# Adding x to the mixed sums on GpSimd alone, from batch 3 on

## The chip, the cores and the metric

One core of one Trainium2 chip runs the kernel. The metric is the device time of one execution in microseconds (us). The engines are named as the profile names them: PE (TensorE, matmuls), PEld (its weight loads), DVE (VectorE), ACT (ScalarE), POOL (GpSimd) and SP (SyncE, which here only issues DMAs). POOL issues DMAs too.

## What is computed

```python
batch, n_heads, seq, head_dim = (8, 12, 448, 64)            # d_model 768, hidden 3072
scores = scale * np.matmul(q, k.transpose(0, 1, 3, 2))
attn = np.maximum(scores, 0.0) ** 2 / S
x = np.matmul(attn, v)                                       # heads side by side: [8, 448, 768]
mixed = np.real(fft(fft(x, axis=1), axis=2))
u = x + mixed
un = (u - mean(u)) / np.sqrt(var(u) + 1e-06)
out = u + np.maximum(un @ w_ch1, 0.0) @ w_ch2
```

The change touches one line of this, `u = x + mixed`.

## The kernel before

Everything runs on one core, batch by batch, with the stages of neighbouring batches laid into one another so that PE always has something to do.

- **Attention** (`attention`, L834). For each batch PE makes scores (L954, in visits of six matmuls), ACT takes relu of them into `sq` (L967), DVE or ACT squares (L984 or L981), and PE multiplies by v (L822, L827). The result leaves PSUM as `xT` (L686 on ACT or L689 on DVE), and a DMA transpose (L796) makes `xn`, with tokens on partitions. q and k are loaded by POOL (L476, L451), copied by DVE (`qkr`, L583) and turned by SP's DMA transposes (`qkT`, L593). From batch 3 on there is one buffer of q and one of k.
- **Mixing** (`mix`, L1416; `mix_rows`, L1228). DVE folds `xT` by the symmetry of the transform (L760 to L780), PE multiplies with the channel table (L1432), and `mix_rows` does the sequence part, once for each of two chunks of a batch. A chunk is two matmuls (L1240) that give a sum's two halves. ACT copies one half (`qs`, L1252), DVE forms `tp = a + b` and `qs = a - b` (L1255, L1257). These are the parts of two rows of tokens: row 0 is the upper half of the sequence, row 1 its mirror image. For each row the inner function `rows(i)` adds x in two instructions, L1275 for the first 385 columns and L1277 for the other 383, which the mirrored part of the other sum gives. So a chunk has four additions, each 112 or 113 partitions of float32 from two SBUF operands. Before the change row 0 is added on DVE and row 1 on POOL. Then follow the statistics on DVE (L1284, L1285), the root on ACT (L1287), the reciprocal on DVE (L1289, L1290) and the normalised row `un` on ACT (L1303) or POOL (L1300).
- **Stores.** Row 0 goes to DRAM as `utop` and `ntop` from SP (L1338), row 1 as `ubot` and `nbot` by indirect DMAs from POOL (L1341). A row's `u` has one buffer from batch 1 on (`BU`), which comes free when `un` has been made and `u` stored.
- **FFN** (`ffn`, L1874; `joint`, L1733). The normalised rows come back transposed as `unT` (L1380, issued by SP) in groups of 256 tokens. Groups 2 to 7 run L1930 (first product, relu by L1917 on ACT or L1915 on DVE) and L1985 or L2071 (second product, added to u by DVE's L1623). The last four groups run as two joints of two groups each: L1762, with copies by ACT (L1777), sums by DVE (L1782), then L2071. The tokens of group 3 are the last 64 of batch 2 and the first 192 of batch 3.

**What sets the order.** The order on each engine is fixed when the program is built. Every stage is a generator that asks for an engine, a modelled duration, what it waits for and which buffers it takes; `Streams.run` (L102) gives the next place to the stage that could start first, and its rank breaks ties. It keeps one clock for each engine. A duration of type `Port` on POOL also makes a DVE `Port` instruction longer while it runs. So one changed duration or engine shifts all later choices: the order of PE, whether a relu goes to ACT or DVE, the place of a load on POOL. On the chip each engine runs its list strictly in that order.

`WHOLE` is 3 (L215). Below it the two additions of a row are placed as one piece, from it on as two (`next_step`, L218).

Of the kernel before, what the change touches and what calls it, by code (L numbers as in the profile page):

```python
# [149 lines left out]
def need(eng, dur, deps=(), bufs=(), ok=None):  # L150
    return eng, dur, list(deps), list(bufs), ok
# [6 lines left out]
def act(n):  # L158
    return n / 1200 + (0.17 if STAGE[0] else 0.2)


def dve(n):
    return n / 960 + 0.15
# [14 lines left out]
def kernel(  # L178
# [9 lines left out]
    nc = tc.nc  # L188
# [9 lines left out]
    KN = D // 2 + 1  # L198
# [16 lines left out]
    WHOLE = 3  # L215
    JOINTS = list(range(8, NGR, 2))

    def next_step(b, eng, d, e):  # L218

        return e if b < WHOLE else (yield need(eng, d))  # L220
# [752 lines left out]
    def sooner(t, other, d, usual, du):  # L973

        wait = {en: max(t, sch.engine[en]) + sch.queued(en) for en in (other, usual)}
        return wait[other] + d + SPARE < wait[usual] + du
# [18 lines left out]
    def side(b, ch):  # L995

        return ch if b < ONE else 1
# [202 lines left out]
    def turn_rows(un, t, n, idn, c0, w, en, done):  # L1200

        e = yield need("PE", 6 * 0.06, [t], [BS])
        pt = BS.take()
        for m in range(MC):
            nc.tensor.matmul(pt[:, m // 3, m % 3 * 128:m % 3 * 128 + w], lhsT=un[:n, m * 128:(m + 1) * 128],
                             rhs=idn, start=True, stop=True)
        if done is second_un[0]:
            BUN[0].free.append(e)
        e = yield need(en, (act if en == "ACT" else dve)(6 * w), [e + LATENCY["PE"]])
        (nc.scalar.copy if en == "ACT" else nc.vector.tensor_copy)(  # L1210
            groups[1][2][:, :, c0:c0 + w].rearrange("p (h m) w -> p h m w", h=2),
            pt[:, :, 0:384].rearrange("p h (m w) -> p h m w", w=128)[:, :, :, 0:w])
        BS.give(pt, e)
        done.t = e + LATENCY["ACT"]
# [13 lines left out]
    def mix_rows(b, ch, pcs):  # L1228
# [38 lines left out]

        def rows(i):

            eng, en, d = ((nc.vector, "DVE", 2 * dve(KN)), (nc.gpsimd, "POOL", 1.8))[i]  # L1270
            one = b < WHOLE
            e1 = yield need(en, Port(d if one else d / 2), [e + LATENCY["DVE"]] + x_ready[b], [BU[i][side(b, ch)]])
            x = xns[b][:, 2 * i + ch, :]
            u = us[i] = work.tile([128, D], FP32, name="u", tag=("u", "u1")[i] + "AB"[side(b, ch)], bufs=1)
            eng.tensor_tensor(u[:n, 0:KN], ts[i][:n, 0:KN], x[:n, 0:KN], op=ALU.add)  # L1275
            e1 = yield from next_step(b, en, Port(d / 2), e1)
            eng.tensor_tensor(u[:n, KN:D], ts[1 - i][:n, KN - 2:0:-1], x[:n, KN:D], op=ALU.add)  # L1277
            made_u[i].t = e1 + LATENCY[en]
            e1 = yield need("DVE", 2 * dve(D // 2) + 0.2 if one else dve(D // 2), [made_u[i]])
            stats = work.tile([128, 2, 6], FP32, name="stats", tag="stats", bufs=2)  # L1280
            for hf in range(2):
                if hf:
                    e1 = yield from next_step(b, "DVE", dve(D // 2) + 0.2, e1)
                nc.vector.bn_stats(stats[:n, hf, :], u[:n, hf * (D // 2):(hf + 1) * (D // 2)])  # L1284
            nc.vector.bn_aggr(mv[:n, i, :], stats[:n])  # L1285
            e1 = yield need("ACT", 0.25, [e1 + LATENCY["DVE"]])
            nc.scalar.activation(std[:n, i:i + 1], mv[:n, i, 1:2], AF.Sqrt, bias=eps_t[:n])  # L1287
            e1 = yield need("DVE", 0.3, [e1 + LATENCY["ACT"]])
            nc.vector.reciprocal(rstd[:n, i:i + 1], std[:n, i:i + 1])  # L1289
            nc.vector.scalar_tensor_tensor(nmr[:n, i:i + 1], mv[:n, i, 0:1], -1.0, rstd[:n, i:i + 1],  # L1290
                                           op0=ALU.mult, op1=ALU.mult)
            if i == 0:
                taken.t = yield need("SP", 0.0, [e1], [BUN[ch if b < ONE else 0]])
            yield need("SP", 0.0, [e1, taken])
            e1 = max(e1, taken.t) + LATENCY["DVE"]
            en = "ACT" if b == 1 or sooner(e1, "ACT", act(D) - 1.0, "POOL", 1.05) else "POOL"
            e1 = yield need(en, act(D) if en == "ACT" else Port(1.05), [e1])
            un = work.tile([128, D], BF16, name="un", tag=f"un{2 * (ch if b < ONE else 0) + i}", bufs=1)
            if en == "POOL":
                nc.gpsimd.tensor_scalar(un[:n], u[:n], rstd[:n, i:i + 1], nmr[:n, i:i + 1],  # L1300
                                        op0=ALU.mult, op1=ALU.add)
            else:
                nc.scalar.activation(un[:n], u[:n], AF.Identity, bias=nmr[:n, i:i + 1],  # L1303
                                     scale=rstd[:n, i:i + 1])
            uns[b][2 * ch + i] = un
            freed[i].t = e1
            made_un[i].t = e1 + LATENCY[en]
            if b == 1:
                nr, idn, c0, w = ((128, ident, 64, 128), (128, rev[:, 0:127], 64 + HS + 97, 127),
                                 (96, ident[:96, :96], 64 + 128, 96), (97, rev[:97, 31:128], 64 + HS, 97))[2 * ch + i]  # L1310
                sch.add(turn_rows(un, e1 + LATENCY[en], nr, idn, c0, w, ("DVE", "ACT")[i],
                                  second_un[1 + 2 * ch + i]), (1, 0.1))

        for i in range(2):
            sch.add(rows(i), rank)
# [899 lines left out]
```

## Time and profile before

| | us |
|---|---|
| three runs | 566.94, 569.09, 569.48 |
| their median | 569.09 |
| the profiled execution: its span | 566.4 |
| of the span, idle on PE | 9.9 |

The profile gives the profiled execution's span, from its first instruction to its last, and no other time for it. The fastest of the three runs lies 0.5 us above that span.

The profile has a page with busy times by engine, groups of equal instructions with the mean time of one, the idle time ahead of them and what ended it. Beside it there are views of the waits (which engine waited for which line), of stretches of time (busy time of each engine in each), of one line's instructions (shortest, median and longest) and a timeline. A time in a timeline counts from the start of the span. The end of a matmul is modelled, so matmuls of two neighbouring lines overlap by a fraction of a microsecond.

### The profile page before, as it was taken

To read this page: it belongs to the slowest core of one execution; us is meant where nothing else is said; L and a number is where in the kernel's file an instruction comes from. 1 tells how busy PE (TensorE), PEld (TensorE's weight loads), DVE (VectorE), ACT (ScalarE), POOL (GpSimd) and SP (SyncE) were. 2 spreads that over 40 slices of the span, in tenths; PEclk is the share of its full clock that TensorE was granted. 3 is DMA by queue.
4 is the path that set the end of the run, shared out by engine and by line. 5 is a ranking of instruction groups with operands and counts; after the bars stand their busy time and mean duration, and the time that the engine had idled before them with its cause. 6 is when DMAs were issued, how large, how long until landed. Compare 5 with 4: busy or idle time off the path is not lost.

```text
span 566.4 us, 11147 instructions
## 1 busy us (share of the span) xinstructions
PE 556.5 (98%) x4171; PEld 350.1 (62%) x4171; DVE 436.2 (77%) x1016; ACT 318.2 (56%) x536; POOL 195.9 (35%) x281
## 2 busy tenths in 40 slices
PE   7999999999999999999999999999999999999997
PEld 4376556544465455556756757767678688668864
DVE  7976564987789978887997896888899957644762
ACT  5978762676745686585786637638515154015400
POOL 8966225523346234462545545222015000000000
PEclk9999999999999999999999999999999999999999
DMA  9999999979959988899899979956425421231012
GB/s 110 180 209 230 215 215 165 217 144 134 181 96 210 215 117 179 164 187 184 174 163 196 198 121 198 164 123 154 115 65 174 124 75 29 71 127 56 1 57 83
DMA packets 152688, 82.41 MB, mean 146 GB/s; under 512 B 118076, under 2 KB 147900, under 8 KB 152636
## 3 DMA queue, kind: packets, MB, share of 16 engines
q0 software_dynamic: 57056, 33.63, 43.0%
q1 hardware_dynamic: 95580, 48.09, 38.1%
q8 instruction: 32, 0.52, 0.4%
q14 instruction: 20, 0.16, 0.1%
HBM read 62.91 MB, written 26.25 MB: 157 GB/s over the span
## 4 chain that ended last, share of the span: by engine, by line
PE 86%; DMA 5%; DVE 4%; ACT 2%; POOL 1%; issue 1%; DVEq 0%; POOLq 0%; ACTq 0%
PE psF L1930 25%; PE psF L2071 20%; PE psS L1762 8%; PE psS L954 7%; PE psS L2071 5%; DMA kn<-in_k_dram 5%; PE psF L827 5%; PE psF L1985 4%; PE psS L1432 2%; PE psF L1762 2%; PE psF L1958 2%; PE psF L822 1%; PE psF L623 1%; DVE sq L984 1%; PE psS L827 1%
## 5 line engine op out<-in xcount | busy, mean ns | idle before, releaser
L1930 PE MATMUL psF<-unT,w 128*128 128x256 bf16 (+2 forms) x1152 | 165.3, 299 | 0.0
L967 ACT ACTIVATE sq<-psS 128x896 bf16<-128x896 f32 x168 | 144.1, 919 | 31.7 <-PE psS L954 31.2
L1930 PEld LDWEIGHTS <-w 128*128 128x128 bf16 x1152 | 110.9, 98 | 49.6 <-issue 5.2
L984 DVE TENSOR_TENSOR sq<-sq 128x896 bf16<-128x896 bf16 x144 | 88.9, 634 | 13.3 <-ACT sq L967 12.5
L2071 PEld LDWEIGHTS <-hT 128*128 128x128 bf16 x648 | 62.5, 98 | 44.1 <-issue 4.8
L1917 ACT ACTIVATE hT<-psF 128x512 bf16<-128x512 f32 (+2 forms) x121 | 59.6, 508 | 41.1 <-PE psF L1930 40.3
L1623 DVE TENSOR_TENSOR o<-psF,o 128x384 f32<-128x384 f32 (+1 forms) x78 | 42.6, 547 | 24.3 <-PE psF L2071 20.8
L2071 PE MATMUL psF<-w,hT 128*128 128x384 bf16 x336 | 59.7, 326 | 0.6 <-DVE o L1623 0.6
L954 PE MATMUL psS<-qkT 64*128 64x448 bf16 (+1 forms) x336 | 51.5, 354 | 1.0 <-DVE qkT L630 0.8
L1777 ACT COPY copies<-psS 128x256 f32<-128x256 f32 x57 | 19.9, 374 | 53.0 <-PE psS L1762 48.1
L689 DVE TENSOR_SCALAR xT<-psF 128x224 bf16<-128x224 f32 x60 | 20.6, 384 | 26.1 <-PE psF L827 26.1
L1275 POOL TENSOR_TENSOR u<-tp,xn 112x385 f32<-112x385 f32 (+2 forms) x14 | 14.5, 1037 | 72.6 <-DVE tp L1255 48.6
L476 POOL DMA_DIRECT2D qn<-in_q_dram x21 | 15.7, 747 | 57.7 <-DVE qkr L583 50.3
L827 PE MATMUL psF<-sq,vn 128*64 128x448 bf16 x246 | 33.0, 362 | 0.0
L954 PEld LDWEIGHTS <-qkT 64*128 64x128 bf16 (+1 forms) x336 | 12.9, 94 | 32.3 <-issue 26.4
L1762 PEld LDWEIGHTS <-w 128*128 128x128 bf16 x288 | 28.2, 98 | 4.7 <-issue 1.1
L451 POOL DMA_DIRECT2D kn<-in_k_dram x42 | 25.9, 626 | 10.3 <-DMA w<-in_moe_w_ch_dram 6.0
L1284 DVE BATCH_NORM_STATS2 stats<-u 112x6 f32<-112x384 f32 (+2 forms) x56 | 28.7, 543 | 0.8 <-POOL u L1275 0.6
L451 POOL DMA_DIRECT2D vn<-in_v_dram x42 | 26.1, 638 | 6.2 <-DMA w<-in_moe_w_ch_dram 5.4
L476 POOL DMA_DIRECT2D vn<-in_v_dram x24 | 18.9, 789 | 25.5 <-PE psS L954 25.4
L1303 ACT ACTIVATE un<-u,small 112x768 bf16<-112x768 f32 (+2 forms) x22 | 22.0, 1023 | 9.5 <-DVE small L1290 8.4
L1782 DVE CUSTOM_DVE_ANT_0 hT<-psS,copies 128x256 bf16<-128x256 f32 x37 | 15.0, 421 | 14.1 <-PE psS L1762 6.2
(238 smaller groups left out, 946.9 us busy)
## 6 DMA issues: line engine op xcount, KB each, us to landing
out_dram<-o SPq DMA_DIRECT2D x55, 192.0 KB, 2.3
qn<-in_q_dram POOLq DMA_DIRECT2D x21, 224.0 KB, 5.1
vn<-in_v_dram POOLq DMA_DIRECT2D x24, 192.0 KB, 5.6
w<-in_moe_w_ch_dram POOLq DMA_DIRECT2D x12, 384.0 KB, 11.8
w<-in_moe_w_ch_dram POOLq DMA_DIRECT2D x4, 1152.0 KB, 23.4
kn<-in_k_dram POOLq DMA_DIRECT2D x21, 192.0 KB, 5.9
utop<-u SPq DMA_DIRECT2D x12, 336.0 KB, 2.9
o<-utop SPq DMA_DIRECT2D x16, 192.0 KB, 3.7
```

Source lines behind the costliest of these rows:

```text
L451: nc.gpsimd.dma_start(out=t[par * Dh:(par + 1) * Dh, par::2], in_=at)
L476: nc.gpsimd.dma_start(out=to, in_=src[b, hs, 0:rows].rearrange("h (p j) d -> p h (j d)", j=j))
L827: nc.tensor.matmul(av[h * Dh:(h + 1) * Dh, 0:S], lhsT=vn_home[:, at:at + Dh], rhs=sq[:, h, :], start=start, stop=stop, skip_group_check=True)
L954: nc.tensor.matmul(sc[:, h, 0:S].rearrange("k (c q) -> k c q", c=4), lhsT=flat[ps, k0:k0 + KB], rhs=qT[ps, pair], start=True, stop=True)
L967: nc.scalar.activation(r, sc[:, :, 0:S], AF.Relu)
L984: nc.vector.tensor_tensor(r, r, r, op=ALU.mult)
L1284: nc.vector.bn_stats(stats[:n, hf, :], u[:n, hf * (D // 2):(hf + 1) * (D // 2)])
L1623: nc.vector.tensor_tensor(o[:, cols], pc[:, cols], o[:, cols], op=ALU.add)
L1762: nc.tensor.matmul(ps[:, 0:N], lhsT=lhs, rhs=rhs[:, m], start=(start and m == 0), stop=(stop and m == 2), skip_group_check=True)
L1917: nc.scalar.activation(hs, ps, AF.Relu)
L1930: nc.tensor.matmul(ph[:, i * N:(i + 1) * N], lhsT=w1_sb[m][hf][:, (jj + i) * 128:(jj + i + 1) * 128], rhs=unT[:, m, 0:N], start=(m == 0), ...
L2071: nc.tensor.matmul(pc[:, cols], lhsT=lhs[i], rhs=rhs[i][:, cols], start=(start and i == 0), stop=(i == KP - 1), skip_group_check=True)
```

## The change

In `rows(i)` the engine of a row's additions was chosen by the row alone. Now it is so only for batches below 3; from batch 3 on both rows take the second choice, POOL, with the modelled time of 1.8 us for a row's two additions.

```diff
         def rows(i):
 
-            eng, en, d = ((nc.vector, "DVE", 2 * dve(KN)), (nc.gpsimd, "POOL", 1.8))[i]
+            eng, en, d = ((nc.vector, "DVE", 2 * dve(KN)), (nc.gpsimd, "POOL", 1.8))[i if b < WHOLE else 1]
             one = b < WHOLE
             e1 = yield need(en, Port(d if one else d / 2), [e + LATENCY["DVE"]] + x_ready[b], [BU[i][side(b, ch)]])
             x = xns[b][:, 2 * i + ch, :]
...
             eng.tensor_tensor(u[:n, 0:KN], ts[i][:n, 0:KN], x[:n, 0:KN], op=ALU.add)
             e1 = yield from next_step(b, en, Port(d / 2), e1)
             eng.tensor_tensor(u[:n, KN:D], ts[1 - i][:n, KN - 2:0:-1], x[:n, KN:D], op=ALU.add)
```

Five batches of two chunks are concerned, so 20 additions change engines. What the planner made of it is seen in the order of the program's instructions.

**POOL, second chunk of batch 3.** `u`, `tp` and `qs` are this chunk's; `nbot3` and `ubot3` are the stores of batch 3, `vn`, `kn` and `qn` loads for later attention. Before:

```order
L451 DMA kn_119<-in_k_dram 64x2x64 x2
L1275 TENSOR_TENSOR u_3336<-tp_3241,xn_2538 112x385
L1341 DMA nbot3_97<-un_3326,backs_105 384x768
L1277 TENSOR_TENSOR u_3336<-qs_3214,xn_2538 112x383
L1341 DMA ubot3_80<-u_3336,backs_105 384x768
L476 DMA vn_120<-in_v_dram 128x4x192
L451 DMA vn_120<-in_v_dram 64x2x64 x2
L1300 TENSOR_SCALAR un_3431<-u_3338,small_3253 112x768
L476 DMA qn_3447<-in_q_dram 112x4x256
```

After:

```order
L476 DMA vn_120<-in_v_dram 128x4x192
L451 DMA vn_120<-in_v_dram 64x2x64
L1341 DMA nbot3_97<-un_3355,backs_105 384x768
L1275 TENSOR_TENSOR u_3376<-qs_3191,xn_2538 112x385
L1277 TENSOR_TENSOR u_3376<-tp_3204,xn_2538 112x383
L1275 TENSOR_TENSOR u_3404<-tp_3204,xn_2538 112x385
L1277 TENSOR_TENSOR u_3404<-qs_3191,xn_2538 112x383
L451 DMA vn_120<-in_v_dram 64x2x64
L1341 DMA ubot3_80<-u_3404,backs_105 384x768
L476 DMA qn_3493<-in_q_dram 112x4x256
```

Four additions now follow each other where two stood around an indirect store. The normalised row that POOL made here (L1300) has gone to ACT.

**SP, the transposes of batch 3's rows.** `ntop3` and `nbot3` are the normalised rows, `unT` the tile of groups 3 and 4 (the transpose of 192 tokens is group 3's), `qkT` q and k for attention, `xn` batch 4's x. Before:

```order
L1338 DMA ntop3_89<-un_3431 112x768
L796 DMA_TRANSPOSE xn_3380<-xT1_108 128x4x128
L1603 DMA out_0_dram<-o_3059 128x384
L593 DMA_TRANSPOSE qkT_3508<-qkr_3426 128x8x112
L1380 DMA_TRANSPOSE unT_3273<-ntop3_89 128x6x192
L1380 DMA_TRANSPOSE unT_3273<-ntop3_89 128x6x32
L1380 DMA_TRANSPOSE unT_3273<-nbot3_97 128x6x224
L796 DMA_TRANSPOSE xn_3380<-xT1_108 128x4x128
L593 DMA_TRANSPOSE qkT_3508<-qkr_3433 128x8x128
```

After:

```order
L1338 DMA ntop3_89<-un_3488 112x768
L593 DMA_TRANSPOSE qkT_3507<-qkr_3490 128x8x112
L796 DMA_TRANSPOSE xn_3424<-xT1_108 128x4x128
L1603 DMA out_0_dram<-o_3059 128x384
L593 DMA_TRANSPOSE qkT_3507<-qkr_3498 128x8x128
L1380 DMA_TRANSPOSE unT_3275<-ntop3_89 128x6x192
L1380 DMA_TRANSPOSE unT_3275<-ntop3_89 128x6x32
L1603 DMA out_0_dram<-o_3076 128x384
L1380 DMA_TRANSPOSE unT_3275<-nbot3_97 128x6x224
```

The second half of `qkT` has moved from behind the `unT` transposes to ahead of them.

**DVE, the start of the first joint.** `chan` and `sumx` hold differences of the joint's `unT` tiles, `o` an output of the group before, `hT` the joint's hidden values. A piece of the difference:

```order
 L1705 TENSOR_TENSOR chan_114<-unT 128x768
 L1705 TENSOR_TENSOR chan_115<-unT,chan_114 128x768
-L1782 ISA hT<-psS,copies 128x256 x2
+L1623 TENSOR_TENSOR o<-psF,o 128x384
 L1705 TENSOR_TENSOR chan_116<-unT 128x768
-L1782 ISA hT<-psS,copies 128x256
+L1705 TENSOR_TENSOR sumx<-unT,chan_115 128x768
+L1623 TENSOR_TENSOR o<-psF,o 128x384 x3
+L1782 ISA hT<-psS,copies 128x256 x3
```

The differences are now made ahead of the joint, among the last additions of group 7, and no longer between its first sums.

The whole program has the same matmuls as before. Beside the 20 additions, the planner moves ten copies out of PSUM (L686 to L689) and three relus (L1917 to L1915) from ACT to DVE, two squares (L984 to L981) from DVE to ACT, and three normalised rows (L1300 to L1303) from POOL to ACT.

## The prediction

> **What bounds the kernel now.** I read the page first, then the stretches that the change can reach, then what PE waits for in them.
>
> ```profile
> span 566.4 us, 11147 instructions
> ...
> PE 556.5 (98%) x4171; PEld 350.1 (62%) x4171; DVE 436.2 (77%) x1016; ACT 318.2 (56%) x536; POOL 195.9 (35%) x281
> ...
> PE 86%; DMA 5%; DVE 4%; ACT 2%; POOL 1%; issue 1%; DVEq 0%; POOLq 0%; ACTq 0%
> ```
>
> PE is busy for 98% of the span and has 86% of the chain that ended last; DVE has 4%. The additions that move are those of batches 3 to 7, all later than 200 us; nothing before is touched. The view of stretches, with busy time and instructions of PE, PEld, DVE, ACT and POOL:
>
> ```profile
> 200.00:440.00 240.00, 239.14 (x1819) 156.35 (x1818) 205.58 (x460) 150.26 (x245) 94.54 (x111) 1.00 0.87 158
> 452.00:506.70 54.70, 54.70 (x420) 40.80 (x418) 33.59 (x86) 16.32 (x48) 0.00 (x0) 1.00 0.25 72
> 506.70:562.60 55.90, 55.31 (x432) 41.64 (x430) 30.38 (x79) 16.29 (x48) 0.00 (x0) 1.00 0.18 57
> ```
>
> The rows are the stretch with all ten chunks, the first joint and the second. PE lacks 0.86 us of 240, nothing in the first joint and 0.59 us in the second. The view of waits, PE alone from 200 us on, names them all:
>
> ```profile
> PE psF L2071 <- DVE o L1623: 0.9, 2, 0.6
> PE psS L1762 <- DVE hT L1782: 0.5, 2, 0.3
> ```
>
> **PE is the bound**, and all the time it loses to others after 200 us is 0.9 + 0.5 = 1.4 us. That is the most that a lighter DVE can give back. A measurement of this kernel tells a change from none at about 0.5%, 2.8 us.
>
> **The change, part by part.**
>
> *PE.* It has the same matmuls in another order, at the same clock (1.00 in the rows above). Cost 0, as long as nothing is late.
>
> *DVE.* It loses 20 additions. These rows of the view of groups are all of them after 200 us (count, busy us, mean ns):
>
> ```profile
> L1275 DVE TENSOR_TENSOR u<-qs,xn 113x385 f32<-113x385 f32 x5 | 4.9, 979 | 0.2
> L1277 DVE TENSOR_TENSOR u<-tp,xn 112x383 f32<-112x383 f32 x5 | 4.6, 911 | 0.0
> L1275 DVE TENSOR_TENSOR u<-qs,xn 112x385 f32<-112x385 f32 x5 | 4.0, 810 | 0.0
> L1277 DVE TENSOR_TENSOR u<-tp,xn 113x383 f32<-113x383 f32 x5 | 4.0, 803 | 0.0
> ```
>
> DVE sheds 4.9 + 4.6 + 4.0 + 4.0 = 17.5 us. The planner spends part of that again, as the order shows: ten copies L689 and three relus L1915 come over from ACT, two squares L984 leave.
>
> ```profile
> L984 DVE TENSOR_TENSOR sq<-sq 128x896 bf16<-128x896 bf16 x144 | 88.9, 634 | 13.3 <-ACT sq L967 12.5
> ...
> L689 DVE TENSOR_SCALAR xT<-psF 128x224 bf16<-128x224 f32 x60 | 20.6, 384 | 26.1 <-PE psF L827 26.1
> ...
> L1915 DVE TENSOR_SCALAR hT<-psF 128x512 bf16<-128x512 f32 x14 | 9.6, 689 | 1.7 <-PE psF L1930 1.5
> ```
>
> That is 10 x 0.384 + 3 x 0.689 - 2 x 0.634 = 4.6 us, so DVE is lighter by 12.9 us of the 205.6 in its stretch. What this is worth on PE lies between 0 and the 0.9 us that PE waits for L1623. I take **-0.4**, about half. The joint's waits for L1782 stand where no addition runs, so they stay.
>
> *POOL.* Shortest, median and longest of its additions after 200 us, and the normalised rows that leave it:
>
> ```profile
> L1275 POOL TENSOR_TENSOR u<-tp,xn x10: 913/917/1652, 221.2 to 432.5; 113x385 f32<-113x385 f32 x5, 112x385 f32<-112x385 f32 x5
> ...
> L1277 POOL TENSOR_TENSOR u<-qs,xn x10: 832/862/1232, 222.1 to 434.6; 113x383 f32<-113x383 f32 x5, 112x383 f32<-112x383 f32 x5
> ...
> L1300 POOL TENSOR_SCALAR un<-u,small 112x768 bf16<-112x768 f32 x3 | 6.0, 2003 | 4.9 <-DVE small L1289 3.8 <-DVE small L1290 1.0
> ...
> L1300 POOL TENSOR_SCALAR un<-u,small 113x768 bf16<-113x768 f32 x3 | 4.2, 1387 | 12.8 <-DVE small L1290 9.7 <-issue 3.1
> ```
>
> It gains 10 x 0.917 + 10 x 0.862 = 17.8 us by the medians, 28.8 by the longest, and sheds three of six `un` at (6.0 + 4.2) / 6 = 1.7, 5.1 us. So it goes from 94.5 us of 240 to between 107 and 118, and is never the bound by its sum. Its queue is the question. POOL's loads of q, k and v now stand behind four additions: 4 x 0.89 = 3.6 us in a row instead of 1.8.
>
> How the pair ran side by side, in the timeline of batch 3's first chunk:
>
> ```profile
> 221.20 0.91 POOL L1275 TENSOR_TENSOR u<-tp,xn 113x385 f32<-113x385 f32 x1 [8.03 <-DMA o<-ubot]
> ...
> 221.74 0.79 DVE L1275 TENSOR_TENSOR u<-qs,xn 113x385 f32<-113x385 f32 x1
> ...
> 222.07 1.15 POOL L1277 TENSOR_TENSOR u<-qs,xn 113x383 f32<-113x383 f32 x1
> 222.45 1.19 DVE L1277 TENSOR_TENSOR u<-tp,xn 113x383 f32<-113x383 f32 x1
> ```
>
> DVE's L1277 takes 1.19 us beside POOL and 0.55 in the quiet case below: the two engines delay each other when both add from SBUF. Alone on POOL, row 0 is done after 1.8 us where DVE needed 1.9, and row 1 after 3.6 instead of 2.0.
>
> The Trainium skill (SBUF — State Buffer, section "Who interferes with whom") says that a DVE instruction with two SBUF inputs and a GpSimd instruction that reads SBUF exclude each other for the whole of one. The 1.19 us agree: the instruction starts 0.77 us before POOL's ends and is 0.64 too long. By that rule each of 20 more POOL additions can hold a DVE addition or square for its 0.89 us, 17.8 us in all, which takes back all that DVE sheds; the -0.4 would go and the forecast would be 0.4 higher.
>
> *What is late next: group 3 of the FFN.* It is the only group that is read soon after it is written. The rows on its path (SP's store of `ntop`, the `unT` transposes, PE's first L1930 of the group at 262.80, DVE's additions of that chunk):
>
> ```profile
> 246.50 0.40 SPq L1338 DMA_DIRECT2D ntop<-un  x1
> ...
> 250.10 1.32 SPq L593 DMA_TRANSPOSE qkT<-qkr  x1
> 253.47 3.06 SPq L1380 DMA_TRANSPOSE unT<-ntop  x2
> ...
> DMA to landing us min/median/max: 2.3/3.4/6.9
> ...
> 262.80 1.47 PE L1930 MATMUL psF<-unT,w 128*128 128x256 bf16 x12
> 264.11 0.35 PE L822 MATMUL psF<-sq,vn 128*128 128x448 bf16 x1
> ...
> 265.08 0.74 PE L954 MATMUL psS<-qkT 64*128 64x448 bf16 x6
> 265.75 1.48 PE L1930 MATMUL psF<-unT,w 128*128 128x256 bf16 x12
> ...
> 260.96 2.00 PE psS L1432 x24
> ...
> 236.04 0.55 DVE L1275 TENSOR_TENSOR u<-qs,xn 112x385 f32<-112x385 f32 x1
> 236.51 0.55 DVE L1277 TENSOR_TENSOR u<-tp,xn 112x383 f32<-112x383 f32 x1
> ```
>
> Group 3 needs the first transpose, issued at 253.47. It lands 2.3 to 6.9 us later, at 255.8 to 260.4, and PE starts at 262.8: 2.4 to 7.0 us to spare. After the change PE has more to do between the second chunk's mixing and group 3: two value visits (265.08 - 264.11 = 0.97 each) and ten scores (10/6 of 0.67) are new, 24 matmuls of L1432 go behind the group's start (2.0, the chain's row): 1.1 us more room, by the order of the matmuls and their pace here. Against it: row 0's additions take 1.8 us where DVE took 1.0 (236.04 to 237.06), and one more `qkT` transpose stands ahead on SP, 1.3 us. The spare is then 1.4 to 6.0 us, so I take **0** here. Every other group that the change reaches has over 55 us of PE work between mixing and use, in the new order too.
>
> *The first joint.* Its matmuls now stand in the order of the second joint's, which lost 0.59 us where the first lost none. Between 0 and 0.6, I take **+0.6**.
>
> *The loads behind four additions.* In the same chunk the load of q started at 245.08 and DVE copied it at 261.47:
>
> ```profile
> 245.08 0.77 POOL L476 DMA_DIRECT2D qn<-in_q_dram  x1
> ...
> 261.47 0.42 DVE L583 COPY qkr<-qn 112x1024 bf16<-112x1024 bf16 x1
> ...
> qn<-in_q_dram POOLq DMA_DIRECT2D x21, 224.0 KB, 5.1
> ```
>
> Less 5.1 us to land, 11 us are to spare, so 1.8 us more on POOL are covered. If that cover goes, they go to PE as they are.
>
> *New short waits.* POOL's longer stretch makes DVE instructions beside it longer by up to 0.64 us at other places than before. Between 0 and ten chunks x 0.6 = 6 us; the nearest row is the stage as it runs now, with 0.9 us in two such waits. I take **+0.8**.
>
> **Sum:** -0.4 + 0 + 0.6 + 0.8 = **+1.0 us** on the profiled execution, 566.4 to 567.4 of span. The three runs have a median of 569.09, 2.7 above that span; carried over, the forecast is **570.1**.
>
> **The rivals.**
> - *Relief.* DVE's 12.9 us give back all PE waits and no new ones come: -1.4, 567.7. For it: both waits name DVE. Against it: they end by 0.3 to 0.6 us each, in an order that is no longer the same.
> - *Many short waits.* Half of the bound above, 3 us, with the joint's 0.6 and without the gain: 572.7. For it: the longer rows beside POOL. Against it: DVE idles for 34 us of that stretch and PE hardly ever waited for it.
> - *Group 3 is late* (slower). Its `un` moves from POOL to ACT's queue, between the relus of scores. These come in threes, 8.4 us apart:
>
> ```profile
> 232.16 2.54 ACT L967 ACTIVATE sq<-psS 128x896 bf16<-128x896 f32 x3 [0.69 <-PE psS L954]
> ...
> 240.59 2.53 ACT L967 ACTIVATE sq<-psS 128x896 bf16<-128x896 f32 x3
> ```
>
>   If `un` slips behind one more three, 8.4 us less the spare of 1.4 to 6.0 reach PE, 2.4 to 7.0 and in the middle 4.7; with the sum's 1.0 the time is 574.8. It decides from a delay of 1.4 us on, at the group's first L1930.
>
> **How the numbers follow.** The forecast has 0.64, relief 0.08, many short waits 0.16, group 3 late 0.12. The forecast's own range is 567.7 to 571.9. The range reaches to 575.3 for group 3's middle and down to 567.2, below relief by the spread of the runs. Slower by over 0.5% (above 571.9) takes the last two but for 0.02, 0.26; faster by over 0.5% (below 566.2) would need twice what PE loses, 0.03; 0.71 are left for within.
>
> **What would show it.** In the changed profile POOL's additions stand in fours of 0.83 to 0.92 us; DVE's busy time falls by 5 to 13 us and PE's does not; the waits of PE after 200 us add up to 1 to 4 us; the first joint takes 55 to 56 us. An L1930 that waits for a DMA near 264 us is group 3 late. Waits of PE for L1623, L984 or L583 of several microseconds would make the prediction wrong, as would PE work that moved behind the second joint.

## The result, and the profile after

| | us |
|---|---|
| after, median of 4 runs | 575.45 (575.07 to 576.05) |
| before, median of 4 runs beside them | 568.62 (566.94 to 569.48) |
| ratio, 95% interval | 1.013 (1.0112 to 1.0147) |
| span of the profiled execution, before and after | 566.4 and 573.1 |

The change costs 6.8 us where 1.0 was forecast. First the page of the changed kernel: span, busy times, and the chain of work that ended last by engine.

```profile
span 573.1 us, 11135 instructions
...
PE 558.4 (97%) x4171; PEld 350.1 (61%) x4171; DVE 431.2 (75%) x1007; ACT 319.6 (56%) x528; POOL 208.9 (36%) x298
...
PE 74%; DMA 10%; DVE 6%; POOL 4%; issue 2%; ACT 2%; SPq 1%; DVEq 0%; POOLq 0%; ACTq 0%
```

PE is still the bound, but has 74% of the chain instead of 86; DMA has doubled to 10%. The move itself went as reckoned on POOL, which gained 208.9 - 195.9 = 13.0 us (12.7 by the medians were expected). DVE lost only 436.2 - 431.2 = 5.0 where 12.9 were expected, because other instructions of its own became longer. The squares (L984) show it best, from 200 us to the first joint, before and after (count, busy us, mean ns):

```profile
L984 DVE TENSOR_TENSOR sq<-sq 128x896 bf16<-128x896 bf16 x70 | 44.1, 646 | 5.6 <-ACT sq L967 5.2
...
L984 DVE TENSOR_TENSOR sq<-sq 128x896 bf16<-128x896 bf16 x68 | 46.2, 690 | 5.9 <-ACT sq L967 5.7
```

Next the view of stretches, cut at the same work in both kernels: from 200 us to the first joint's first matmul, the first joint, the second joint. The columns are length, then busy time of PE, PEld, DVE, ACT and POOL. Before:

```profile
200.00:451.55 251.55, 250.69 (x1891) 163.30 (x1889) 216.76 (x485) 152.03 (x246) 95.47 (x112) 1.00 0.85 155
451.55:506.51 54.96, 54.96 (x421) 41.02 (x420) 34.04 (x87) 16.32 (x48) 0.00 (x0) 1.00 0.25 73
506.51:562.54 56.03, 55.50 (x434) 41.82 (x431) 30.36 (x78) 16.29 (x48) 0.00 (x0) 1.00 0.18 58
```

After:

```profile
200.00:456.87 256.87, 251.52 (x1889) 163.02 (x1888) 212.87 (x479) 153.01 (x238) 107.41 (x129) 1.00 0.86 152
456.87:512.19 55.32, 55.07 (x422) 41.08 (x420) 32.58 (x82) 16.91 (x48) 0.00 (x0) 1.00 0.26 72
512.19:569.21 57.02, 55.80 (x434) 41.80 (x431) 30.60 (x78) 16.15 (x48) 0.00 (x0) 1.00 0.18 57
```

The three stretches are longer by 5.32, 0.36 and 0.99 us, together 6.67: all of the span's 6.7. In the first one PE is idle for 256.87 - 251.52 = 5.35 us, where it was idle for 0.86. The view of waits, PE alone from 200 us on, says for what (the rows of 0.4 us and more):

```profile
PE psS L954 <- DMA qkT<-qkr: 3.1, 1, 3.1
PE psF L1985 <- DVE xT L689: 0.7, 1, 0.7
PE psS L1762 <- DVE hT L1782: 0.6, 2, 0.3
PE psF L2071 <- ACT hT L1917: 0.4, 1, 0.4
PE psF L1930 <- ACT hT L1917: 0.4, 1, 0.4
PE psS L1762 <- ACT copies L1777: 0.4, 2, 0.2
```

Before, PE waited for L1623 and L1782 alone. The largest new wait is one of 3.1 us, by the scores (L954) of batch 6, second of three groups of heads, for a transposed half of q and k. The chain of waits from 300 to 330 us shows what stood ahead of that transpose (start, us, what):

```profile
307.95 0.53 SPq L1603
...
308.57 3.79 SPq L1380
...
312.46 0.53 SPq L1603
...
313.04 4.64 DMA qkT<-qkr
317.68 0.04 issue
317.73 0.36 PE psS L954 x2
```

SP was issuing `unT<-ntop` (L1380, rows of batch 4) for 3.79 us and an output store before it came to `qkT` at 313.04; the data landed at 317.68, and PE went on. In the kernel before, SP's timeline has the two the other way round (the last row is PE's):

```profile
305.56 1.70 SPq L593 DMA_TRANSPOSE qkT<-qkr  x1
307.36 0.78 SPq L1603 DMA_DIRECT2D out_dram<-o  x1
308.22 2.48 SPq L1380 DMA_TRANSPOSE unT<-ntop  x1
...
313.00 0.74 PE L954 MATMUL psS<-qkT 64*128 64x448 bf16 x6
```

There `qkT` was issued at 305.56, and the visit of scores that meets it began at 313.00. In the changed kernel the first four of that visit run at 314.06 and the last two wait, so the last two are what needs this half. So the first reading is that **the new order, not the engine that adds, costs the time**.

### The profile page after: what moved, and what is told of

Same layout as the page of the kernel before. It is cut to its first block, busy times and chain, and to the rows that moved or that the text cites. A ratio compares the mean times of both kernels' runs of the same rounds, so it can differ in the third digit from the quotient of the medians.

```text
span 573.1 us, 11135 instructions
## 1 busy us (share of the span) xinstructions
PE 558.4 (97%) x4171; PEld 350.1 (61%) x4171; DVE 431.2 (75%) x1007; ACT 319.6 (56%) x528; POOL 208.9 (36%) x298
## 4 chain that ended last, share of the span: by engine, by line
PE 74%; DMA 10%; DVE 6%; POOL 4%; issue 2%; ACT 2%; SPq 1%; DVEq 0%; POOLq 0%; ACTq 0%
PE psF L1930 20%; PE psF L2071 19%; PE psS L2071 7%; PE psS L1762 7%; PE psS L954 5%; DMA kn<-in_k_dram 5%; PE psF L1985 4%; DMA w<-in_moe_w_ch_dram 4%; PE psF L827 3%; PE psF L1762 2%; PE psS L1432 2%; PE psF L1958 2%; DVE stats L1284 1%; PE psF L822 1%; DVE sq L984 1%
## 5 line engine op out<-in xcount | busy, mean ns | idle before, releaser
L967 ACT ACTIVATE sq<-psS 128x896 bf16<-128x896 f32 x168 | 143.6, 917 | 47.0 <-PE psS L954 46.7
L984 DVE TENSOR_TENSOR sq<-sq 128x896 bf16<-128x896 bf16 x142 | 90.9, 655 | 13.6 <-ACT sq L967 13.0
L1917 ACT ACTIVATE hT<-psF 128x512 bf16<-128x512 f32 (+2 forms) x118 | 58.1, 509 | 43.5 <-PE psF L1930 42.8
L954 PE MATMUL psS<-qkT 64*128 64x448 bf16 (+1 forms) x336 | 51.6, 355 | 4.0 <-DMA qkT<-qkr 3.1
L1623 DVE TENSOR_TENSOR o<-psF,o 128x384 f32<-128x384 f32 (+1 forms) x73 | 39.6, 543 | 18.4 <-PE psF L2071 13.7
L2071 PE MATMUL psF<-w,hT 128*128 128x384 bf16 x294 | 51.8, 326 | 0.4 <-ACT hT L1917 0.4
L1777 ACT COPY copies<-psS 128x256 f32<-128x256 f32 x48 | 17.3, 375 | 56.0 <-DVE o L1623 24.8
L689 DVE TENSOR_SCALAR xT<-psF 128x224 bf16<-128x224 f32 x64 | 21.8, 383 | 23.5 <-PE psF L827 23.5
L954 PEld LDWEIGHTS <-qkT 64*128 64x128 bf16 (+1 forms) x336 | 12.9, 94 | 35.3 <-issue 26.5
L1275 POOL TENSOR_TENSOR u<-qs,xn 113x385 f32<-113x385 f32 (+1 forms) x10 | 9.6, 957 | 58.1 <-issue 31.6
L1303 ACT ACTIVATE un<-u,small 112x768 bf16<-112x768 f32 (+2 forms) x25 | 25.1, 1023 | 10.0 <-DVE small L1290 9.0
L1284 DVE BATCH_NORM_STATS2 stats<-u 112x6 f32<-112x384 f32 (+2 forms) x56 | 29.4, 545 | 1.3 <-POOL u L1275 0.9
L451 POOL DMA_DIRECT2D kn<-in_k_dram x42 | 25.9, 624 | 10.6 <-PE psS L954 9.1
L476 POOL DMA_DIRECT2D kn<-in_k_dram x21 | 16.2, 772 | 28.1 <-DVE qkr L583 20.6
```

The lines of the kernel that those rows point to most:

```text
L451: nc.gpsimd.dma_start(out=t[par * Dh:(par + 1) * Dh, par::2], in_=at)
L476: nc.gpsimd.dma_start(out=to, in_=src[b, hs, 0:rows].rearrange("h (p j) d -> p h (j d)", j=j))
L954: nc.tensor.matmul(sc[:, h, 0:S].rearrange("k (c q) -> k c q", c=4), lhsT=flat[ps, k0:k0 + KB], rhs=qT[ps, pair], start=True, stop=True)
L967: nc.scalar.activation(r, sc[:, :, 0:S], AF.Relu)
L984: nc.vector.tensor_tensor(r, r, r, op=ALU.mult)
L1623: nc.vector.tensor_tensor(o[:, cols], pc[:, cols], o[:, cols], op=ALU.add)
```

## The experiments

**Theory O (order):** the planner lays out another program once the additions have another engine, and this layout puts work late, on SP above all. **Rival E (engine):** twenty more POOL additions themselves cost the time, by their length or by what they hold up on DVE. Each run below is timed beside runs of the kernel before on the same chip.

### Engine and order apart

`engine_alone` keeps the planner's view of before and only issues the twenty additions on POOL. `order_alone` does the opposite: the planner reckons as in the changed kernel, but row 0 is added by DVE. PE, ACT and SP keep the order of before in the first and that of the changed kernel in the second.

```diff
 engine_alone, on the kernel before, behind L1270:
+            eng = nc.gpsimd if b >= WHOLE else eng
 order_alone, on the changed kernel, behind L1270:
+            eng = nc.vector if i == 0 else eng
```

> The planner reckons as before (row 0 on DVE), and the 20 additions from batch 3 on are issued on POOL all the same. PE, ACT and SP keep the order of before word for word; DVE loses 20 rows and POOL gets them at their old place in time. Theory O (the new order costs the time): within 1.5 us of before, 567 to 570, and no wait of PE for qkT. Theory E (the additions on POOL cost it, by POOL's queue or by holding up DVE): 5 us or more over before, 573 to 576.

> The planner reckons as after the change (row 0 on POOL), and row 0 is added on DVE all the same. PE, ACT and SP have the order of after word for word. Theory O: 5 to 7 us over before, 573.5 to 576, with PE's wait of about 3 us for the qkT of batch 6's second group near 314 us and some 1.2 us more in the joints than before. Theory E: within 1.5 us of before.

| | before's order | changed order |
|---|---|---|
| row 0 on DVE | 568.0 (before) | 576.75, ratio 1.0143 (1.0119 to 1.0167) |
| both rows on POOL | 570.32, ratio 1.004 (1.0024 to 1.0056) | 575.45, ratio 1.013 (1.0112 to 1.0147) |

The order costs 8.7 us with the old engines, 5.1 with the new. The engine costs 2.3 us in before's order; in the order made for it the medians differ by 1.3 the other way, and the intervals overlap. The order has the larger share by far, but the engine's 2.3 us are real. `engine_alone` ended 0.3 us above the range of theory O and far below that of E; `order_alone` 0.8 above that of O. Not all of the 8.7 us is order alone: in `order_alone` PE waits 1.93 us at 344.53 for an L1623 that stands behind one of DVE's own additions, which took 2.73 us beside POOL's two, and PE's clock fell behind its longest wait (last section), which it did not in the changed kernel's profile. DVE's waits from 200 to 440 us in `engine_alone` point to the engine's cost:

```profile
DVE stats L1284 <- POOL u L1275: 6.7, 7, 2.1
DVE stats L1284 <- POOL u L1277: 6.0, 8, 1.1
```

DVE runs its list in order, and the statistics of row 0, placed where DVE's own additions had been finished, now stand at its head waiting for POOL, 12.7 us in all. Everything behind them waits too: L1284 waits 1.02 us until 240.93, a copy out of PSUM (L689) stands behind it, and PE waits 0.83 us for that copy until 243.47. All of PE's waits for DVE after 200 us add up to 2.9 us in this run, where before has 1.4. In the changed kernel the planner knew and put L1284 later; the same two rows read:

```profile
DVE stats L1284 <- POOL u L1277: 0.2, 1, 0.2
DVE stats L1284 <- POOL u L1275: 0.2, 1, 0.2
```

### The transpose on SP

`sp_fix` is the changed kernel with one more dependence for the planner: the transpose of batch 4's upper rows (L1380, part 5) waits for the issue of the second half of `qkT` of batch 6, second group. Only SP's order changes.

```diff
-                    e = sch.dma(e + 0.5, R * 2048, 180e3)
+                    issued[b][g].t, e = e if x else None, sch.dma(e + 0.5, R * 2048, 180e3)
...
-                deps = [c.t + STORED for c in n[half::2]]
+                deps = [c.t + STORED for c in n[half::2]] + ([issued[6][1]] if k == 5 else [])
```

> The changed kernel with one difference: on SP the second half of qkT for batch 6's second group, and one store of out, stand ahead of the transpose of batch 4's normalised rows instead of behind it. Theory O with SP's queue as the place: PE's wait for qkT near 314 us goes from 3.1 us to under 0.5, and the time falls by 2.5 to 3.4 us, to 572 to 573. Rival (the wait only moves, to the transposed rows or to the next scores): 574.5 to 576.

It takes 573.2 us, ratio 1.0099 (1.0081 to 1.0118): 2.3 us less than the changed kernel by the medians, 2.8 by the spans (573.1 and 570.3), and 1.8 by the two ratios to before, whose intervals just overlap. PE's wait is down to what this row says:

```profile
PE psS L954 <- DMA qkT<-qkr: 0.3, 1, 0.3
```

So SP's order cost 1.8 to 2.8 us of the 6.8. In the two profiles the wait of 3.1 went to the end almost whole.

### The joints, and other plans with the old engines

`before_d20` and `before_d16` leave row 0 on DVE and only change the duration that the planner reckons for a row on POOL, 2.0 or 1.6 us instead of 1.8, from batch 3 on. `b7_only` moves row 0 to POOL in batch 7 alone.

```diff
 before_d20 (2.0) and before_d16 (1.6), on the kernel before:
-            eng, en, d = ((nc.vector, "DVE", 2 * dve(KN)), (nc.gpsimd, "POOL", 1.8))[i]
+            eng, en, d = ((nc.vector, "DVE", 2 * dve(KN)), (nc.gpsimd, "POOL", 1.8 if b < WHOLE else 2.0))[i]
 b7_only, on the changed kernel:
-... [i if b < WHOLE else 1]
+... [i if b < 7 else 1]
```

> The kernel before, with the modelled time of POOL's two additions of a row from batch 3 on at 2.0 instead of 1.8 us: same engines, another order from there on. Theory O': any re-planned order finds places that the model has wrong, so 1 to 6 us over before. Rival (re-planning is free as such; only this change's order is bad): within 1 us of before, 567.5 to 570.

> The kernel before (row 0 on DVE, row 1 on POOL) with POOL's modelled 1.8 us lowered to 1.6 in batches 3 to 7: same engines, another order. Theory O: any other order costs something against the one of before; with 2.0 it was +4.0; here +1 to +5, 569 to 573. Rival (the order of before is nothing special, and a layout with the old engines gives 568 again): within 0.7 us of before.

> Both rows on POOL in batch 7 only; in all other batches as before. Up to the second chunk of batch 7 the order of every engine is that of before, SP keeps its transposes of batches 3 to 6 where they were, and the first joint (L1762) gets the order that it has in the changed kernel. Theory J (the joint's order costs its share whatever engine adds x): in-joint stalls of PE as in the changed kernel, about 2.0 to 2.4 us in both joints instead of 1.2, so +1.0 to +1.5 on before, 569 to 570. Rival (the joint's extra stalls come from being reached late or from the earlier batches' state): no more than 1.2 us of stalls in the joints, time within 0.5 us of before.

The times are 572.03 (1.0075, 1.0057 to 1.0093), 572.63 (1.0094, 1.0069 to 1.0119) and 570.09 (1.0048, 1.0031 to 1.0066). So a plan made anew costs 4 to 5 us with not one addition moved, and the order of before is better than either neighbour. The two joints of `b7_only` in the view of stretches:

```profile
452.00:507.32 55.32, 55.07 (x422) 41.09 (x420) 32.60 (x82) 16.86 (x48) 0.00 (x0) 1.00 0.26 72
507.32:564.35 57.03, 55.81 (x434) 41.79 (x431) 30.63 (x78) 16.15 (x48) 0.00 (x0) 1.00 0.18 57
```

They are the lengths of the changed kernel, 55.32 and 57.02, and `before_d20` has 55.32 and 57.02 as well, while `engine_alone`, with before's order, has before's 54.96 and 56.03. The joints' 1.35 us therefore go with the order, whoever adds. `b7_only` came out 1.2 us slower than expected by that alone; its trace has a wait of that length which before does not have, though no run shows that it is the whole difference:

```profile
PE psF L1930 <- ACT hT L1917: 1.2, 1, 1.2
```

### Other plans with the new engines

If the order alone decided, another plan with all twenty additions on POOL should land anywhere. `after_d16` and `after_d20` are the changed kernel with the same two durations.

> The changed kernel with POOL's modelled 1.8 us for a row's two additions lowered to 1.6 in batches 3 to 7: all twenty additions still on POOL, but the planner lays out another order. On SP the halves of qkT for batch 6, group 2 stand together, as in before. Theory O (the time hangs on the order, not on who adds): no wait of scores for qkT above 0.5 us, so 2.5 to 4 us below the changed kernel, 571 to 573; what remains is joints and short waits. Rival E (twenty additions more on POOL cost the time): 575 to 576, as the changed kernel.

> The changed kernel with POOL's modelled 1.8 us raised to 2.0 in batches 3 to 7, a third order with all twenty additions on POOL. On SP the second half of qkT for batch 6, group 2 again stands right behind the first. Theory O: the wait of scores for qkT is gone, and the time lands among those of the other re-planned orders, 570 to 574. Rival E: 575 to 576.

| planner's duration | 1.6 | 1.8 | 2.0 |
|---|---|---|---|
| row 0 on DVE | 572.63 | 568.62 | 572.03 |
| both rows on POOL | 578.16 (1.0191, 1.0172 to 1.021) | 575.45 | 579.54 (1.0199, 1.0174 to 1.0224) |

No theory's number held: the late `qkT` is gone at its old place, and yet both kernels are slower still. (The trace of `after_d20` is of the longest of its five executions, 584.96 us; the other four took 577.60 to 579.93.) In each column the change costs 5.5 to 7.5 us, by the medians. Theory O in its simple form, that any plan is as good as another, falls. The timeline of `after_d16` shows a wait of another kind (POOL, DVE and PE):

```profile
340.30 1.05 POOL L1341 DMA_INDIRECT nbot<-un,backs  x1 [0.30 <-issue]
341.38 0.92 POOL L1275 TENSOR_TENSOR u<-qs,xn 112x385 f32<-112x385 f32 x1
342.26 0.85 POOL L1277 TENSOR_TENSOR u<-tp,xn 112x383 f32<-112x383 f32 x1
343.06 0.91 POOL L1275 TENSOR_TENSOR u<-tp,xn 112x385 f32<-112x385 f32 x1
343.93 0.83 POOL L1277 TENSOR_TENSOR u<-qs,xn 112x383 f32<-112x383 f32 x1
...
341.10 4.15 DVE L984 TENSOR_TENSOR sq<-sq 128x896 bf16<-128x896 bf16 x1 [0.18 <-ACT sq L967]
345.17 0.55 DVE L1623 TENSOR_TENSOR o<-psF,o 128x384 f32<-128x384 f32 x1
...
345.77 0.48 PE L2071 MATMUL psF<-wsum,hT 128*128 128x384 bf16 x2 [2.55 <-DVE o L1623]
```

A square on DVE, 0.62 us as a rule, starts at 341.10, 0.28 us ahead of the first addition, and ends at 345.25, 0.5 us after the last of POOL's four additions. L1623 stands behind it, and PE waits 2.55 us for L1623. The same happens at 284.58 (4.15 us), where PE waits for the square itself, and in `after_d20` at 240.53, 289.21 (a fold of `xT`, L762) and 338.28.

### What a run of four additions holds up

Three edits of `after_d16` test this. `d16_gap` puts a one-column memset behind each POOL addition, `d16_split` issues one tiny load (64 rows of two elements, never read) between the two rows of a chunk, `d16_row0` gives row 0 back to DVE. PE, ACT and SP keep their order in all three. `d20_gap` and `d20_split` do the first two in `after_d20`, `after_gap` the first in the changed kernel.

```diff
 gap: behind L1275 and L1277
+            if b >= WHOLE: nc.gpsimd.memset(spare, 0.0)
 split: ahead of L1275
+            if i and b >= WHOLE: nc.gpsimd.dma_start(out=spare, in_=q[0, 0, 0:64, 0:2])
 d16_row0: behind L1270
+            eng = nc.vector if i == 0 else eng
```

> The order of after_d16 on every engine; on POOL a one-column memset of a spare tile stands behind each of the forty additions of batches 3 to 7. In after_d16 a square on DVE (L984) that started beside POOL's run of four additions took 4.15 us at 284.6 and again at 341.1 (0.62 is its usual time) and ended with the run; PE waited 1.5 and 2.6 us behind them. Theory H (POOL does not give way between additions that follow each other at once, so the square is held for the whole run): the memset lets it in after one addition, it takes 1.0 to 1.6 us, PE's waits for L984 and for L1623 fall from 4.7 us to below 1.5, and the time falls by 2.5 to 4 us against after_d16, to 574 to 575.7. Rival R (the square is slowed for as long as POOL works on SBUF, whatever stands between): it keeps 4 us or more, the time stays at 578.

> The same memsets in the order of after_d20, where DVE instructions were held for 4.12 us at 240.5, 3.49 at 289.2 and 4.58 at 338.3, and PE waited 1.8, 1.1 and 2.7 us near the first and the last. Theory H: no DVE instruction beside the additions above 1.7 us, 3 to 5 us less than after_d20, 574.5 to 576.5. Rival R: 578 to 580.

> The same memsets in the changed kernel, where one square was held, 3.59 us at 289.05, with no wait of PE of over 0.3 us in the 17 us behind it. Theory H: that square falls to below 1.7 us, and PE gains nothing to speak of, 0 to 0.7 us, 574.7 to 575.5, since the wait of 3.1 us for qkT stays. Rival (the held square is what put qkT late): that wait falls by 1 us or more, time 574 or less.

> The order of after_d16 on every engine; on POOL one small load of a spare tile (64 rows of two elements, read by nobody) is issued between the two rows' additions of each chunk of batches 3 to 7, so that the run of four becomes two runs of two with about 0.7 us of issue between. Memsets of 0.1 us in the same places let nothing through. Theory H2 (what waits on DVE gets in only where POOL turns to an issue): the squares held 4.15 us take 2.0 to 2.5, PE's waits for L984 and L1623 fall from 4.7 us to 0.5 to 2, and the time falls by 1.5 to 4 us against after_d16, to 574 to 576.7. Rival R (the square is slowed for as long as the chunk's additions last, whatever stands between): 4.5 us or more per square, time 578 or above.

> The same loads in the order of after_d20. Theory H2: the three DVE instructions held 4.12, 3.49 and 4.58 us take at most 2.9, time 1.5 to 4 us below after_d20, 575.5 to 578. Rival R: 579 or above.

> The order of after_d16, with row 0's additions issued on DVE at their places (as order_alone did it in the changed kernel's order). Theory O (the order costs the time whoever adds): within 2 us of after_d16, 576 to 580, with DVE's own additions taking 1.2 to 2.7 us beside POOL's two. Theory H2 with the engine as cause: squares held no longer than 2 us, 574 to 575.5.

The memset lets nothing through: the held instructions took 4.22, 3.55 and 4.67 us in `d20_gap`, and 3.79 in `after_gap`. The same square as above in `d16_gap`, with the first of the memsets:

```profile
343.27 0.94 POOL L1275 TENSOR_TENSOR u<-qs,xn 112x385 f32<-112x385 f32 x1
344.13 0.12 POOL L1267 MEMSET spare<- 128x1 f32 x1
...
343.00 4.26 DVE L984 TENSOR_TENSOR sq<-sq 128x896 bf16<-128x896 bf16 x1 [0.18 <-ACT sq L967]
```

The issue of a load does. In `d16_split`:

```profile
348.07 0.85 POOL L1277 TENSOR_TENSOR u<-tp,xn 112x383 f32<-112x383 f32 x1
348.85 0.57 POOL L1267 DMA_DIRECT2D spare<-in_q_dram  x1
349.44 1.07 POOL L1275 TENSOR_TENSOR u<-tp,xn 112x385 f32<-112x385 f32 x1
...
346.91 2.83 DVE L984 TENSOR_TENSOR sq<-sq 128x896 bf16<-128x896 bf16 x1 [0.18 <-ACT sq L967]
...
350.26 0.97 PE L2071 MATMUL psF<-wsum,hT 128*128 128x384 bf16 x5 [1.23 <-DVE o L1623]
```

The square ends at 349.74, inside POOL's next addition, which took 1.07 instead of 0.91. It was held for two additions, not four, and PE's wait fell from 2.55 to 1.23. At the other places the hold is shorter too: 2.93 us instead of 4.15 in `d16_split`; 3.10, 2.24 and 3.19 instead of 4.12, 3.49 and 4.58 in `d20_split`. That much of the mechanism is shown, though H2 had expected 2.0 to 2.5 us in the first plan and at most 2.9 in the second. What in the issue lets the square in is not shown: it also leaves a longer gap than the memset, 0.57 us against 0.12. The time was not bought back:

| | us | ratio, interval | PE waits there |
|---|---|---|---|
| `after_d16` | 578.16 | 1.0191 (1.0172 to 1.021) | 2.6 for L1623, 1.5 for L984 |
| `d16_gap` | 579.59 | 1.0195 (1.0156 to 1.0233) | 2.7, 1.7 |
| `d16_split` | 581.47 | 1.0232 (1.0206 to 1.0257) | 1.2, 0.3, but new: 2.5 for L1451, 1.0 for L967 |
| `d16_row0` | 575.49 | 1.0134 (1.0109 to 1.0159) | 1.9 for L1277 |
| `d20_gap` | 582.27 | 1.0244 (1.0217 to 1.027) | as `after_d20`, without its 1.6 for `qkT` |
| `d20_split` | 581.07 | 1.0237 (1.0191 to 1.0284) | 1.3 instead of 2.5 for L1623, but 3.5 instead of 1.6 for `qkT` |
| `after_gap` | 574.77 | 1.0114 (1.0089 to 1.0139) | 2.9 for `qkT`, as the changed kernel |

Both splits took the time of rival R (578 or above, 579 or above). New waits stand elsewhere in their traces, which the ten loads may have caused, so their time says nothing of the hold; only the held instruction and PE's wait behind it do. `d16_row0` is the measure of the engine in this plan: 578.16 - 575.49 = 2.7 us, at the end of what H2 expected and 0.5 below the range of O. DVE's own addition is held there in turn, for POOL's two:

```profile
337.57 2.71 DVE L1275 TENSOR_TENSOR u<-qs,xn 112x385 f32<-112x385 f32 x1
```

So the engine costs 2.3 us in before's order, 2.7 in that of `after_d16` and nothing that can be measured in the changed kernel's; the order costs, with row 0 on DVE and against the kernel before, 8.7 us (changed kernel) and 575.49 - 567.88 = 7.6 (`after_d16`). In the changed kernel itself one square was held for long:

```profile
L984 DVE TENSOR_TENSOR sq<-sq x68: 570/617/3589, 200.1 to 406.9; 128x896 bf16<-128x896 bf16 x68
```

It is the one at 289.05, 3.59 us. From 286 to 305 us the view of waits has no row for PE, so here the hold cost nothing that the trace shows. In `after_gap` that square still took 3.79 us, and the wait for `qkT` stayed. None of the plans tried beats the kernel before.

## Why the prediction was wrong

- **The step that failed** is the search for what is late, behind "Cost 0, as long as nothing is late". It looked at two places, both in batch 3: group 3, and in "the loads behind four additions" the load of q, from POOL's issue to DVE's copy, 11 us to spare, cost 0. The way from that copy through SP's transpose to the scores had no term of its own, and there the time went. (The sentence that every other group has over 55 us is about the FFN's groups; no wait of PE for `unT` contradicts it.) SP's queue was looked at in batch 3, where `qkT` had moved ahead of the `unT` transposes. A batch later it had moved behind one, past the longest transpose issue on SP (3.79 us), and its own issue came 313.04 - 305.56 = 7.5 us later. The margin of before was small: the two scores that need it ran at about 313.4 (four of the visit's six first, an estimate), which less the issue at 305.56 and 4.8 us of median landing time leaves about 3.0 us. PE itself came 1.1 us later (314.06 for 313.00). So 7.5 - 3.0 - 1.1 = 3.4 us should be missing, and the trace has 3.1. `sp_fix` gives that term in time: 1.8 to 2.8 us.
- **The first joint, +0.6**: right in kind and too small. The first joint lost 0.36. The second was taken as unchanged and lost 0.99. `b7_only` and `before_d20` have the same 1.35 in the two.
- **New short waits, +0.8**: 5.32 us of the first stretch less the 2.8 that `sp_fix` returns leave 2.5 net. PE's idle time there grew by 4.5 us, 3.1 of them for `qkT`; the other 1.4 are waits of 0.7 us and less. The other 0.8 of the stretch is busy time of PE (250.69 and 251.52), for which no run gives a cause. The bound of 6 held, the choice was low by 0.6 by the waits and by 1.7 by the stretch. Why each of the waits came was not tried one by one.
- **Relief, -0.4**: DVE got lighter by 5.0 us in the changed kernel, not by 12.9, and its lighter load was worth nothing where the order stood still: `engine_alone` lost 2.3 us, since statistics that had waited for nothing now waited for POOL. The prediction asked who waits for DVE, and not for whom DVE waits. In the changed order the engine made no measurable difference, so the price depends on the plan.
- **Group 3, 0**: right, with some luck. Its first matmul came at 263.56 us instead of 262.80, and no wait for a DMA stands there. But its transpose was issued at 258.69 instead of 253.47 and landed 3.7 us later, 1.2 us before its use, which is below the reckoned 1.4 to 6.0. Other `unT` transposes of that trace took up to 7.6 us to land.
- **POOL, 0**: right by its sum, 13.0 us for 12.7.
- **The rule on shared access to SBUF** was priced as 17.8 us of holds that only take back what DVE sheds. In the changed kernel DVE's busy time fell by 7.9 us less than reckoned (12.9 - 5.0). The Trainium skill (SBUF — State Buffer, section "Who interferes with whom") has an instruction block the other engine's for the whole of one instruction. The runs agree that it blocks, but the hold was as long as the whole run: 3.59 us in the changed kernel and up to 4.58 in `after_d20`, against 0.92 for one addition. The rule also says that a GpSimd instruction that only writes does not contend; a memset of 0.1 us between the additions let nothing in all the same.

Of the rivals, "group 3 is late", given 0.12, came near the measured time (574.8 and 575.45), but by chance. It shares with the runs that a transpose reaches its consumer too late. Its delay was to come from ACT's queue, at group 3, and to cost 4.7 us; the one that came was on SP, at the scores of batch 6, and cost 1.8 to 2.8. By spans the loss is 2.8 for SP's order, 1.35 for the joints and 2.5 that is the rest.

What stays open is why each of the three plans with the additions on POOL is 5.5 to 7.5 us slower than its neighbour with row 0 on DVE. The holds are part of it in `after_d16`, where giving row 0 back to DVE returns 2.7 us; in `after_d20` they stand ahead of PE's longest waits, but no run gives their price. In `after_d16` the rest, 575.49 - 572.63 = 2.9 us, goes with the order; the waits differ from plan to plan.

## What to carry to other kernels

Where a program's order is planned from modelled durations, price an edit twice: the instructions themselves, and the plan made anew. Here the second was the larger, and re-planning with no addition moved already cost 4 to 5 us. For the second, go along every in-order queue over the whole reach of the change, SP's too, and look for a transfer that has moved behind a long issue; its margin before the change, not the engine's load, says what that costs. And when work moves from a busy engine to a free one, look at what on the busy one uses the result next: it can block that queue. In `engine_alone` DVE's 12.7 us of new waits stood against the 17.5 us of work that it shed.

## What the hardware did that had not been expected

- A DVE instruction with two SBUF operands that meets a run of POOL additions can be held to the end of the run: 3.49 to 4.67 us for runs of three and four, 2.24 to 3.19 where an issue stood in the middle. It is not so each time; in the same traces DVE and POOL also took turns, with POOL's additions lengthened to between 1.0 and 1.7 us. What decides between the two was not found.
- The issue of a DMA transpose occupied SP for 1.2 to 3.8 us in the changed kernel's trace, and the queue behind it stood for as long.
- The clock that PE was granted halved behind some waits. In `order_alone`, where PE waited 2.46 us until 316.02, the view of stretches has a clock (the figure behind POOL's count) of 0.65 and then 0.50:

```profile
316.00:318.00 2.00, 1.98 (x12) 1.33 (x13) 0.43 (x1) 0.92 (x1) 1.19 (x2) 0.65 1.26 264
318.00:320.00 2.00, 2.00 (x10) 1.41 (x9) 1.16 (x3) 0.49 (x1) 0.76 (x2) 0.50 0.89 184
```

  By these rows the wait cost some 0.7 + 1.0 = 1.7 us more than its own length (an estimate). In `after_d20` the clock was 0.50 from 345 to 347 us, behind a wait of 2.51. In the changed kernel's profile it stayed at 1.00 behind the wait of 3.11, so the length of a wait alone does not decide it.
